# A convolution and squared-ReLU kernel: the tokens' scales as one row on every partition, applied ahead of the turning

## The chip, the cores and the metric

The kernel runs on one core of a Trainium2 chip. The metric is the device time of one execution in microseconds (us), here the median of three runs. A core has five engines with queues of their own that work side by side: TensorE (PE, matrix products; its weight loads are shown apart as PEld), VectorE (DVE), ScalarE (ACT), GpSimd (POOL) and SyncE (SP), which in this kernel issues every DMA. The transfers themselves run on 16 DMA engines.

## The reference

Eight sequences of 4096 tokens with 192 channels go through a convolution whose seven weights are made per token and head by a softmax, and then through a two-layer network with a squared ReLU between the layers:

```python
w = exp(weight_gen - max(weight_gen, -1)); w = w / (sum(w, -1) + 1e-9)   # [B, S, 8, 7]
x_unf = windows of 7 tokens ending at s, zeros ahead of token 0           # [B, S, 7, 8, 24]
out = einsum('bshk,bskhg->bshg', w, x_unf).reshape(B * S, 192)
h = out @ w_in                    # [32768, 192] @ [192, 2048]
r = maximum(h, 0.0)
result = ((r * r) @ w_out)        # [32768, 2048] @ [2048, 192], float32
```

Inputs and output are 32-bit floats (the network's two weight matrices arrive in 64 bits).

## The kernel before

**Tiling.** Partition p holds 256 consecutive tokens. A chunk `c` is four tokens of every partition (512 tokens); there are 64 chunks, and two chunks make a group `gi`, whose inputs one `load_group` brings in. Each matrix product is done with 16-bit operands: a number is split into a high and a low part (`xh`, `xl`; `gh`, `gl`; W and V hold split weights), and three products of parts are summed in PSUM.

**A chunk's path.** DVE makes the softmax weights and the seven products and sums of the convolution (`conv_steps`, L316 and L322). From chunk 4 on DVE also turns the sums in 32x32 blocks (L404), they go to DRAM and back (`xd`, L410 and L415), and arrive as `xT` with channels on partitions. ACT and DVE split `xT` into `xh` and `xl` (L356, L362). `mm1` (L440) makes the hidden layer in PSUM, ACT does ReLU, square and the high part (L447, L451, L455), DVE the low part (L459), and `mm2_turned` (L485, L489) multiplies by V. `finish` takes the sums out of PSUM to the tile `s` (L531 on ACT, L532 on DVE); `store_turned` turns `s` into `o_sb` (L548), multiplies by the tokens' scales (L550), and issues 24 stores of 16 KB (L557), whose pieces are 32 floats, 128 bytes.

**Turned chunks.** For chunks 4 to 62 (`turned(c)`) the products come out with channels on partitions and tokens along the row, so `s` is [128, 768] with 128 tokens in each of six blocks. Chunks 0 to 3 and 63 have tokens on partitions and take the scale as one number per partition, `falls[gi]` (L543, L544).

**The scales.** Each group's inputs are scaled by a power of two per partition, `ups`, and the output is brought back by `f`, which `descale(gi)` makes from `downs` and the weights' scale `back` (L152): one number for each of the 128 partitions, that is for each token place of a turned chunk. For groups 2 to 31 (30 groups) `descale` writes the 128 numbers from 128 partitions to a DRAM row `fd` of 512 bytes (L156), and reads them back four times (L158), once for each block of 32 partitions, so that partition i of a block has the numbers i, 32+i, 64+i and 96+i: the tile `fs`, [128, 4], which after the turning is what each output number needs.

**Order.** It is written out by hand. The loop at the end of the kernel runs over chunks and eight steps `b` in each: two `mm1`, the late low parts, `finish` and `store_turned` of the chunk before (at `b == 1`), a piece of `mm2`, then ACT's steps, then what `todo` holds for that step. `descale(gi)` stands there some three chunks ahead of the first chunk of its group. All DMAs stand in SP's one queue in the order in which they are written, and an instruction of SP that waits holds those behind it.

Of the kernel before, what the change touches and what calls it, by code (L numbers as in the profile page):

```python
# [8 lines left out]
F32 = mybir.dt.float32  # L9
# [4 lines left out]
ALU = mybir.AluOpType  # L14
# [15 lines left out]
def kernel(  # L30
# [9 lines left out]
    nc = tc.nc  # L40
# [4 lines left out]
    P = 128  # L45
    Q = 32
# [6 lines left out]
    CPG = TG // TC  # L53
# [8 lines left out]
    N_PE = 4  # L62
# [4 lines left out]
    att = ctx.enter_context(tc.tile_pool(name="att", bufs=1))  # L67
    xtp = ctx.enter_context(tc.tile_pool(name="xtp", bufs=2))
    gp = ctx.enter_context(tc.tile_pool(name="gp", bufs=4))
    op = ctx.enter_context(tc.tile_pool(name="op", bufs=2))  # L70
    dram = ctx.enter_context(tc.tile_pool(name="dram", bufs=2, space=bass.MemoryType.DRAM))
# [15 lines left out]
    back = const.tile([P, 1], F32, name="back")  # L87
# [3 lines left out]
    act, ts, tt = nc.scalar.activation, nc.vector.tensor_scalar, nc.vector.tensor_tensor  # L91
    stt = nc.vector.scalar_tensor_tensor
# [33 lines left out]
    sums, ups, downs, falls = {}, {}, {}, {}  # L126
# [20 lines left out]
    spread_falls = {}  # L147

    def descale(gi):
        f = falls[gi] = att.tile([P, 1], F32, name="f", bufs=3)  # L150
        d = downs.pop(gi)
        stt(out=f, in0=d, scalar=back, in1=d, op0=ALU.mult, op1=ALU.mult)  # L152
        if gi * CPG >= N_PE:
            fd = dram.tile([P], F32, name="fd")
            fs = spread_falls[gi] = att.tile([P, 1, P // Q, 1], F32, name="fs", bufs=3)
            nc.sync.dma_start(out=fd.rearrange("(p a) -> p a", a=1), in_=f)  # L156
            for m in range(P // Q):
                nc.sync.dma_start(  # L158
                    out=fs[m * Q:(m + 1) * Q, 0, :, 0], in_=fd.rearrange("(q i) -> i q", i=Q)
                )  # L160

    raws = {}

# [259 lines left out]
    def turned(c):  # L423
        return N_PE <= c < NCH - 1
# [96 lines left out]
    outs, sums_t = {}, {}  # L521
# [23 lines left out]

    def store_turned(c):
        o = op.tile([P, TC * D], F32, name="o_sb")
        nc.vector.transpose(o, sums_t.pop(c))  # L548
        ob = o.rearrange("p (a q j) -> p a q j", q=P // Q, j=Q)
        tt(out=ob, in0=ob, in1=spread_falls[c // CPG].broadcast_to(ob.shape), op=ALU.mult)  # L550
        for col in range(0, D, Q):
            for t in range(TC):
                if col < P:
                    p0, n0 = col, t * P
                else:
                    p0, n0 = 2 * t // TC * D1 + col - P, N + t % 2 * P
                nc.sync.dma_start(  # L557
                    out=out_v[:, c * TC + t, col:col + Q].rearrange("(q i) j -> i q j", i=Q),
                    in_=o[p0:p0 + Q, n0:n0 + P].rearrange("i (q j) -> i q j", j=Q),
                )  # L560
# [122 lines left out]
    cvt[NU][1]()  # L683
    cvt[NU][2]()
    descale(0)
    descale(1)
    for f in conv2[3:6]:
        f()
# [37 lines left out]
    for c in range(1, NCH + 1):  # L726
        for b in range(NB if c < NCH else 2):
            js = (2 * b, 2 * b + 1)
            if c < NCH:
                if b == 0 and c % 2 and (c + 3) // 2 * CPG < NCH:  # L730
                    load_group((c + 3) // 2)
                if c % 2 and b == 2 and (c + 3) // 2 * CPG < NCH:
                    total, scales = size_steps((c + 3) // 2)
                    b1 = 4 if c == 1 else 2
                    at(c, b1, total)
                    at(c, b1 + 1, scales)
                    at(c, b1 + 1, lambda gi=(c + 3) // 2: descale(gi))
                if b == 0 and c + 2 < NCH and c + 2 > 2:
                    plan_conv(c + 2)
                for j in js:  # L740
                    mm1(c, j)
# [6 lines left out]
            if b == 1:  # L748
                for p in range(2):
                    finish(c - 1, p)  # L750
                    if c == NCH:
                        store(c - 1, p, p + 1)
                if turned(c - 1):
                    store_turned(c - 1)
                elif c < NCH:
                    store(c - 1)
# [55 lines left out]
```

## Time and profile before

| | |
|---|---|
| median of three runs (2076.53 to 2078.67) | 2078.55 us |
| the profiled execution's own time | 2084.55 us |
| its span, first to last instruction | 2082.8 us |
| mean granted TensorE clock | 0.995 |
| busy: PE, PEld | 98%, 84% of the span |
| busy: DVE, ACT, POOL | 90%, 84%, 0% of the span |
| DMA: mean rate, share of the 16 engines that the kernel's queue used | 77 GB/s, 30.2% |

A row of a group of instructions reads: line, engine, operation, output<-inputs, shapes, count, then busy time in us, mean ns of one, and the engine's idle time just before them with what ended it. "issue" as a releaser means that the engine waited for nothing that the profile shows. In a row of a table by stretches of time, each engine's busy us (and number of instructions) stand in order PE, PEld, DVE, ACT, POOL, then the granted clock as a share of full speed, the share of the DMA engines and GB/s. In the list of DMA queues, q1 is the kernel's own transfers and q8, called "instruction", the loading of the engines' instructions.

### The profile page before, as it was taken

The numbers are of one execution on the slowest core, as the hardware profiler recorded it, in microseconds if no ns is written. First come the engines' busy times: TensorE is split into PE (matmuls) and PEld (weight loads), VectorE is DVE, ScalarE is ACT, GpSimd is POOL, SyncE is SP. The second block draws the span as 40 slices with busy tenths as digits, with TensorE's granted clock in tenths as the row PEclk, the third lists the DMA queues.
The fourth block names the chain that finished last, engine by engine and source line by source line (L and its number), as shares of the span: only waits on it lengthen the run. The fifth ranks groups of instructions, "written<-read, shape, count | busy, mean of one in ns | idle before, by whom it ended". The sixth has DMA issues, their size and how long they took to land.

```text
span 2082.8 us, 92659 instructions
## 1 busy us (share of the span) xinstructions
PE 2047.9 (98%) x42310; PEld 1744.4 (84%) x42310; DVE 1864.4 (90%) x2428; ACT 1750.4 (84%) x2010; POOL 10.2 (0%) x14
## 2 busy tenths in 40 slices
PE   8999999999999999999999999999999999999999
PEld 6776666678988889998888999998999988889886
DVE  8998999989999998999898999998899999999983
ACT  6788888878888888888888888887888888888887
POOL 1000000000000000000000000000000000000000
PEclk9999999999999999999999999999999999999999
DMA  6122233332323322233323233323332232332221
GB/s 183 40 71 69 56 83 79 95 81 49 86 68 94 92 75 61 66 85 94 85 60 73 68 95 90 76 56 86 72 92 74 55 89 70 94 90 72 59 59 23
DMA packets 315162, 159.71 MB, mean 77 GB/s; under 512 B 232729, under 2 KB 285337, under 8 KB 310801
## 3 DMA queue, kind: packets, MB, share of 16 engines
q1 hardware_dynamic: 314768, 153.79, 30.2%
q8 instruction: 330, 5.41, 1.3%
q14 instruction: 64, 0.52, 0.1%
HBM read 104.88 MB, written 48.77 MB: 74 GB/s over the span
## 4 chain that ended last, share of the span: by engine, by line
PE 95%; DVE 3%; issue 1%; SPq 0%; DMA 0%; ACT 0%; POOL 0%; DVEq 0%; POOLq 0%
PE ph L440 48%; PE acc L485 34%; PE acc L489 9%; PE acc L513 3%; DVE pr L316 1%; DVE pr L322 0%; DVE du L208 0%; DVE du L209 0%; DVE du L207 0%; PE ph L385 0%; DVE W L272 0%; SPq L117 0%; DMA xt<-in_x_dram 0%; DVE gl L459 0%; DVE xl L362 0%
## 5 line engine op out<-in xcount | busy, mean ns | idle before, releaser
L440 PEld LDWEIGHTS <-W 64*64 64x64 f16 (+1 forms) x17568 | 762.5, 107 | 208.7 <-issue 4.5
L440 PE MATMUL ph<-xh,W 64*64 64x512 f16 (+1 forms) x11712 | 882.7, 377 | 0.8 <-DVE xl L362 0.5
L485 PE MATMUL acc<-gh,V 64*64 64x512 f16 x7552 | 805.6, 377 | 13.4 <-issue 13.4
L459 DVE SCALAR_TENSOR_TENSOR gl<-gh,g 128x1024 f16<-128x1024 f16 x504 | 611.6, 1223 | 142.9 <-ACT gh L455 133.1
L447 ACT ACTIVATE g<-ph 128x1024 f32<-128x1024 f32 x504 | 511.9, 1016 | 258.0 <-PE ph L440 257.9
L485 PEld LDWEIGHTS <-V 64*64 64x64 f16 x11328 | 645.9, 107 | 76.1 <-issue 17.7
L489 PE MATMUL acc<-gh,V 64*64 64x256 f16 x7552 | 696.7, 270 | 4.1 <-issue 4.0
L489 PEld LDWEIGHTS <-V 64*64 64x64 f16 x11328 | 645.2, 107 | 22.7 <-issue 10.2
L451 ACT ACTIVATE g<-g 128x1024 f32<-128x1024 f32 x512 | 539.3, 1053 | 8.0
L455 ACT ACTIVATE gh<-g 128x1024 f16<-128x1024 f32 x504 | 530.7, 1053 | 8.0
L485 PE MATMUL acc<-gl,V 64*64 64x512 f16 x3776 | 497.8, 378 | 2.5 <-issue 2.5
L440 PE MATMUL ph<-xl,W 64*64 64x512 f16 (+1 forms) x5856 | 477.7, 377 | 0.0
L316 DVE TENSOR_TENSOR pr<-xt,wt 128x768 f32<-128x768 f32 x449 | 422.1, 953 | 2.8 <-DMA xt<-in_x_dram 0.7
L489 PE MATMUL acc<-gl,V 64*64 64x256 f16 x3776 | 395.7, 270 | 1.3 <-issue 1.3
L322 DVE TENSOR_TENSOR pr<-pr 128x768 f32<-128x768 f32 x384 | 365.3, 951 | 2.3
L362 DVE TENSOR_TENSOR xl<-xT,xh 128x512 f16<-128x512 f32 x180 | 113.5, 686 | 21.6 <-ACT xh L356 20.3
L356 ACT CAST xh<-xT 128x512 f16<-128x512 f32 x180 | 98.7, 611 | 1.2 <-DMA xT<-xd 1.1
L531 ACT COPY tmp<-acc 128x512 f32<-128x512 f32 x118 | 50.0, 475 | 24.3 <-PE acc L485 23.2
L532 DVE TENSOR_TENSOR s<-acc,tmp 128x512 f32<-128x512 f32 x118 | 60.0, 551 | 10.4 <-ACT tmp L531 10.4
L513 PE MATMUL acc<-V,gl 64*128 64x192 f16 x512 | 63.5, 243 | 2.9 <-issue 2.6
L513 PE MATMUL acc<-V,gh 64*128 64x192 f16 x1024 | 65.3, 243 | 0.0
L404 DVE STREAM_TRANSPOSE xr<-pr 128x768 f32<-128x768 f32 x60 | 58.7, 978 | 2.1
(76 smaller groups left out, 646.5 us busy)
## 6 DMA issues: line engine op xcount, KB each, us to landing
xT<-xd SPq DMA_DIRECT2D x120, 384.0 KB, 5.3
xt<-in_x_dram SPq DMA_DIRECT2D x31, 1344.0 KB, 6.9
xd<-xr SPq DMA_DIRECT2D x240, 96.0 KB, 3.5
out_dram<-o_sb SPq DMA_DIRECT2D x1416, 16.0 KB, 2.5
wt<-in_weight_gen_dram SPq DMA_DIRECT2D x31, 224.0 KB, 2.7
raw<-in_moe_w_in_dram SPq DMA_DIRECT2D x8, 384.0 KB
raw<-in_moe_w_out_dram SPq DMA_DIRECT2D x4, 768.0 KB, 4.4
fs<-fd SPq DMA_DIRECT2D x120, 0.5 KB, 4.0
```

The costliest lines, as they stand in the source:

```text
L316: tt(out=dst, in0=src, in1=wk.broadcast_to([P, (t1 - t0) * H, G]), op=ALU.mult)
L322: tt(out=prs[k0][:, part], in0=prs[k0][:, part], in1=prs[k][:, part], op=ALU.add)
L356: nc.scalar.copy(xh, xs)
L362: tt(out=xl, in0=xs, in1=xh, op=ALU.subtract)
L440: nc.tensor.matmul(ph[col, i], w[rows, k, j % 2, col], xx[rows, k], **fl)
L447: act(r, phs.pop((c, j)), AF.Relu, scale=RHO * LIFT ** 0.5)
L451: act(r, r, AF.Square)
L455: act(gh, rgs[c, j], AF.Copy, scale=1.0 / LIFT)
L459: stt(out=gl, in0=ghs[c, j], scalar=-LIFT, in1=rgs.pop((c, j)), op0=ALU.mult, op1=ALU.add)
L485: nc.tensor.matmul(accs[c][0][col, r], V[rows, fb, d:d + D1], g[rows, i], **fl)
L489: nc.tensor.matmul(accs[c][1][col, r, 0:N // 2], V[rows, fb, d:d + D1], g[rows, i, m * N // 2:(m + 1) * N // 2], **fl,)
L513: nc.tensor.matmul(accs[c][t // 2][:, h, t % 2 * D:(t % 2 + 1) * D], g[rows, i, t * P:(t + 1) * P], V[rows, fb, n * D:(n + 1) * D], start= ...
```

## The change

`descale` makes the scales 32 times side by side ([128, 32] instead of [128, 1]) and, for groups 2 to 31, turns that tile in 32x32 blocks on DVE, after which partitions 0, 32, 64 and 96 each hold 32 of the scales as a row. Four stores of one such row (32 floats, 128 bytes) each fill `fd`; one load brings `fd` back as a whole row of 128 numbers to each of the 128 partitions. `store_turned` multiplies `s` by that row, in place, and turns afterwards.

```diff
     def descale(gi):
-        f = falls[gi] = att.tile([P, 1], F32, name="f", bufs=3)
+        row = att.tile([P, Q], F32, name="f", bufs=3)
+        f = falls[gi] = row[:, 0:1]
         d = downs.pop(gi)
-        stt(out=f, in0=d, scalar=back, in1=d, op0=ALU.mult, op1=ALU.mult)
-        if gi * CPG >= N_PE:
-            fd = dram.tile([P], F32, name="fd")
-            fs = spread_falls[gi] = att.tile([P, 1, P // Q, 1], F32, name="fs", bufs=3)
-            nc.sync.dma_start(out=fd.rearrange("(p a) -> p a", a=1), in_=f)
-            for m in range(P // Q):
-                nc.sync.dma_start(
-                    out=fs[m * Q:(m + 1) * Q, 0, :, 0], in_=fd.rearrange("(q i) -> i q", i=Q)
-                )
+        dq = d.broadcast_to([P, Q])
+        stt(out=row, in0=dq, scalar=back, in1=dq, op0=ALU.mult, op1=ALU.mult)
+        if turned(gi * CPG):
+            turned_row = att.tile([P, Q], F32, name="ft", bufs=2)
+            nc.vector.transpose(turned_row, row)
+            fd = dram.tile([P // Q, Q], F32, name="fd")
+            for q in range(P // Q):
+                nc.sync.dma_start(out=fd[q:q + 1], in_=turned_row[q * Q:q * Q + 1, :])
+            fs = spread_falls[gi] = att.tile([P, 1, P], F32, name="fs", bufs=3)
+            nc.sync.dma_start(
+                out=fs[:, 0], in_=fd.rearrange("(a q) i -> a (q i)", a=1).broadcast_to([P, P])
+            )
...
     def store_turned(c):
         o = op.tile([P, TC * D], F32, name="o_sb")
-        nc.vector.transpose(o, sums_t.pop(c))
-        ob = o.rearrange("p (a q j) -> p a q j", q=P // Q, j=Q)
-        tt(out=ob, in0=ob, in1=spread_falls[c // CPG].broadcast_to(ob.shape), op=ALU.mult)
+        sm = sums_t.pop(c)
+        sb = sm.rearrange("p (t n) -> p t n", n=P)
+        tt(out=sb, in0=sb, in1=spread_falls[c // CPG].broadcast_to(sb.shape), op=ALU.mult)
+        nc.vector.transpose(o, sm)
```

The order of PE's and ACT's instructions is as before. On SP, at one group's `descale` (the rows stand between the output stores of one chunk and the DRAM trip of a later one), before:

```order
L557 DMA out_dram<-o_sb 32x4x32 x24
L156 DMA fd<-f 128x1
L158 DMA fs<-fd 32x4x1 x4
L410 DMA xd<-xr 32x6x128 x4
L415 DMA xT<-xd 64x3x512 x2
```

and now:

```order
L562 DMA out_dram<-o_sb 32x4x32 x24
L160 DMA fd<-ft 1x32 x4
L162 DMA fs<-fd 128x128
L414 DMA xd<-xr 32x6x128 x4
L419 DMA xT<-xd 64x3x512 x2
```

One store and four loads have become four stores and one load, at the same place of the queue. On DVE, at the same `descale` (`down` and `up` are the group's powers of two, `gl` the low part of the hidden layer, `pr` the convolution's products), before:

```order
L142 TENSOR_SCALAR down<-down 128x1
L96 TENSOR_SCALAR up<-down 128x1
L97 TENSOR_SCALAR down<-down 128x1
L152 SCALAR_TENSOR_TENSOR f<-down,back 128x1
L459 SCALAR_TENSOR_TENSOR gl<-gh,g 128x1024 x2
```

and now:

```order
L142 TENSOR_SCALAR down<-down 128x1
L96 TENSOR_SCALAR up<-down 128x1
L97 TENSOR_SCALAR down<-down 128x1
L154 SCALAR_TENSOR_TENSOR f<-down,back 128x32
L157 STREAM_TRANSPOSE ft<-f 128x32
L463 SCALAR_TENSOR_TENSOR gl<-gh,g 128x1024 x2
```

The first is wider, and a transpose of [128, 32] has come in behind it. In `store_turned` the two DVE instructions of 128x768 have changed places, the multiplication (L554, formerly L550) now ahead of the transpose (L555, formerly L548).

## The prediction

> **What bounds the kernel now.** I read the page's first part, then the table of waits, then the stretches of time around one group's `descale`, and last the DMA list. The busy times and PE's waits:
>
> ```profile
> PE 2047.9 (98%) x42310; PEld 1744.4 (84%) x42310; DVE 1864.4 (90%) x2428; ACT 1750.4 (84%) x2010; POOL 10.2 (0%) x14
> PE acc L485 <- issue: 15.8, 11, 2.6
> PE acc L489 <- issue: 5.3, 5, 1.9
> PE acc L513 <- issue: 2.6, 1, 2.6
> core 0: 2082.8 us, clock 0.995
> ```
>
> PE is the bound. Behind the start it waits for no other engine to speak of: what it loses is "issue", 15.8 + 5.3 + 2.6 = 23.7 us in 17 gaps of up to 2.6 us, and the clock, which was granted at 0.995 in the mean, 0.005 x 2082.8 = 10.4 us. So the question is where these gaps stand. I cut the time into 30 stretches from 5.5 to 9.5 us behind each issue of the store `fd<-f`, and the 29 stretches between them. Three of the short ones, their sum, the sum of the long ones, and the stretch behind the gap at 424:
>
> ```profile
> 361.10:365.10 4.00, 4.00 (x100) 2.47 (x92) 3.93 (x6) 3.72 (x6) 0.00 (x0) 1.00 0.05 4
> 423.40:427.40 4.00, 2.09 (x41) 1.12 (x33) 3.93 (x6) 2.94 (x4) 0.00 (x0) 0.96 0.00 0
> 805.60:809.60 4.00, 1.37 (x33) 1.08 (x28) 3.93 (x6) 2.93 (x4) 0.00 (x0) 0.97 0.01 4
> sum 120.00, PE 95.82 PEld 77.66 DVE 117.86 ACT 102.02 POOL 0.00; mean PE 3.19 PEld 2.59 DVE 3.93 ACT 3.40 POOL 0.00
> sum 1719.10, PE 1719.10 PEld 1485.60 DVE 1555.19 ACT 1462.48 POOL 0.00; mean PE 59.28 PEld 51.23 DVE 53.63 ACT 50.43 POOL 0.00
> 427.05:430.46 3.41, 3.41 (x44) 2.90 (x48) 1.41 (x3) 0.85 (x2) 0.00 (x0) 0.50 0.04 0
> ```
>
> In the 120 us just ahead of the landing of `fd`, PE is idle for 24.2; in the other 1719.1 us it is never idle. After a gap the clock may stand at half for 3.41 us (last row). Every gap of the steady state thus belongs to the store of the scales. How it does so is seen at 417.90 (SP's and PE's timeline) and in the DMA list of 418.0 to 426.7, followed by the list's rows for the whole run:
>
> ```profile
> 417.90 0.34 SPq L156 DMA_DIRECT2D fd<-f  x1
> 424.34 0.38 PE L485 MATMUL acc<-gl,V 64*64 64x512 f16 x1
> 426.34 0.37 PE L485 MATMUL acc<-gl,V 64*64 64x512 f16 x1 [1.63 <-issue]
> 427.01 1.74 SPq L158 DMA_DIRECT2D fs<-fd  x4
> ...
> DMA packets 145, 0.02 MB, mean 2 GB/s; under 512 B 144, under 2 KB 144, under 8 KB 144
> q8 instruction: 1, 0.02, 2.4%
> q1 hardware_dynamic: 144, 0.00, 0.9%
> ...
> q8 instruction: 330, 5.41, 1.3%
> out_dram<-o_sb SPq DMA_DIRECT2D x1416, 16.0 KB, 2.5
> fs<-fd SPq DMA_DIRECT2D x120, 0.5 KB, 4.0
> fd<-f SPq DMA_DIRECT2D x30, 0.5 KB, 8.7
> ```
>
> The store of 512 bytes takes 8.7 us to land, longer than any other transfer of its size or of 32 times its size: `o_sb` stores 16 KB in pieces of 128 bytes in 2.5 us. Its pieces are 4 bytes (144 packets: 128 and some 16 for the end). Meanwhile the DMA engines move nothing but one packet of instructions, which needs 2.4% of 16 engines over 8.7 us, 3.3 us; over the run 1.3% x 16 x 2082.8 / 330 makes 1.3 us a packet. The 330 packets carry the program's 92,659 instructions, about 280 each; PE executes 48 per us (x100 and x92 in the 4.00 us from 361.10), so a packet is some 6 us of its work. So while the small writes are outstanding instructions are held up, and PE runs dry. The earliest it did:
>
> ```profile
> 800.08 0.34 SPq L156 DMA_DIRECT2D fd<-f  x1
> 808.72 0.42 PE L485 MATMUL acc<-gh,V 64*64 64x512 f16 x2 [2.63 <-issue]
> ```
>
> 808.72 - 2.63 - 800.08 = 6.0 us behind the issue: a hold-up that ends before 6.0 us should cost PE nothing, and one of 8.7 us at most 2.7, as the longest gaps show.
>
> **What the hold-up costs in all.** Rather than add gaps, clock and restarts, I take the distance between issues of `fd`, one group of PE work:
>
> ```profile
> 164.56 0.34 SPq L156 DMA_DIRECT2D fd<-f  x1
> 231.06 0.34 SPq L156 DMA_DIRECT2D fd<-f  x1
> 293.34 0.34 SPq L156 DMA_DIRECT2D fd<-f  x1
> 484.52 0.34 SPq L156 DMA_DIRECT2D fd<-f  x1
> 1948.94 0.34 SPq L156 DMA_DIRECT2D fd<-f  x1
> ```
>
> A group without a gap takes 293.34 - 231.06 = 62.28 us (so do 10 more of the 28); the one from 417.90 to 484.52, with 1.9 us of gaps, takes 66.62. From the first to the last are 28 groups, 1784.38 us; at 62.28 each they would take 1743.84. The loss is 40.5 us: 24.2 idle, about 10 of clock, and some 6 of slow restart around the gaps.
>
> By the Trainium skill (TensorE: Matmul & The Clock Gate, Part 1) the clock falls after an idle window of about 3.4 us; by that rule no gap here would lower it and the loss would be the 30 us of idling and restart, an estimate of 2048.5. The trace differs: the clock was at 0.50 behind a gap of 1.63 us, so the rows decide.
>
> **The change, part by part.** *The stores.* Gone are the 128 pieces of 4 bytes; four stores of one 128-byte piece come instead. The trace has no store from a single partition. The nearest row is `o_sb`, pieces of the same 128 bytes, 2.5 us to landing, though there are 128 of them. At 0.34 us an issue the fourth starts 1.0 us behind the first and lands at about 3.5. From above: if a store to `fd` lands in 8.7 us whatever its pieces, the last lands at about 1.0 + 8.7 = 9.7. I take 3.5, since the piece is the same as `o_sb`'s and during 24 of those stores in a row PE never idles. That is under 6.0, and the stores cost PE nothing.
>
> *The load.* One broadcast of 512 bytes to 128 partitions instead of four gathers that land in 4.0 us at the median. It moves 64 KB in 512-byte pieces; `o_sb`'s quarter of that lands in 2.5. I take 4; it is issued when the stores have landed, so it is done about 8 us behind the first issue. Gathers of the same row run without a gap in the 29 long stretches, which hold them all, so I count no hold-up from reading. `fs` is used some three chunks (over 90 us) later and is not waited for.
>
> *SP's queue* holds what stands behind the load: the next chunk's `xd` and `xT`, and later the output stores. They now wait for the landing of four stores (about 3.5 us) instead of one. How long SP waited before, with the rows for DVE's part:
>
> ```profile
> SPq L158 <- DMA fd<-f: 231.6, 29, 8.7
> ACT xh L356 <- DMA xT<-xd: 1.1, 1, 1.1
> L303 DVE TENSOR_SCALAR sm<-sm 128x32 f32<-128x32 f32 x64 | 11.6, 181 | 2.2
> L152 DVE SCALAR_TENSOR_TENSOR f<-down,back 128x1 f32<-128x1 f32 x32 | 6.9, 220 | 1.1
> L142 DVE TENSOR_SCALAR down<-down 128x1 f32<-128x1 f32 x31 | 4.8, 154 | 1.1
> L548 DVE STREAM_TRANSPOSE o_sb<-s 128x768 f32<-128x768 f32 x59 | 57.7, 978 | 2.0
> L550 DVE TENSOR_TENSOR o_sb<-o_sb,fs 128x768 f32<-128x768 f32 x59 | 56.5, 958 | 2.0
> L316 DVE TENSOR_TENSOR pr<-xt,wt 128x768 f32<-128x768 f32 x447 | 421.1, 955 | 2.8 <-DMA xt<-in_x_dram 0.7
> ```
>
> 231.6 us of SP's waiting shrink by some 4 to 5 us per group. Nobody gains: `xT` was waited for once, 1.1 us. Nor is anything behind it made later.
>
> *DVE.* The scales' instruction grows from 128x1 to 128x32: between L142 (154 ns) and L303 (181) lie the same 31 elements, so 220 becomes about 247. The new transpose of 128x32 costs between 154 ns and the 978 of 128x768; near the small end, 0.2 us. Together 0.23 us in 62.28, 30 x 0.23 = 7 us in all, on an engine that is idle 120 - 117.9 + 1719.1 - 1555.2 = 166 us of these stretches; PE, busy without a break in the long stretches beside it, does not wait for DVE. Were that cover gone, the price would be those 7 us. In `store_turned` a multiplication (958) and a transpose (978) change places; the second operand now repeats in the middle dimension, and L316's (955) repeats inside, so the rate does not depend on that. Zero.
>
> **The sum.** 2084.55 - 40.5 = 2044.0 for the profiled execution. It stands 6.0 us over the median of the runs. If those 6 us are a fixed cost of being profiled, the runs come to 2038; if they are hold-ups that the runs have less of, 2044. Between them 2041; I add 2 for groups in which the stores and the load together still starve PE: **2043 us**.
>
> **The rivals.** *A part remains.* If the load holds instructions up as the store did, the hold-up ends at 8 us instead of 8.7: gaps of at most 2.0 instead of 2.7, and since both their number and their length shrink, about (2.0/2.7) squared = 0.55 of the loss stays, 22 us: 2078.55 - 18.5 = 2060. Against it: the gathers, which hold none up.
>
> *Nothing happens.* The gaps stand where `descale` stands, but something else of that moment could starve PE, the DVE or ACT work around it for one. Then 2078.55. The Trainium skill (Runtime: NRT & Kernel Launch, Instruction fetch mechanics) calls the crossing into the next block of instructions mostly hidden, which speaks for this rival. Against it: a packet of instructions at 3.3 us instead of 1.3, and a gap in the middle of four like products whose operands are there.
>
> *Slower.* The 8.7 us belong to the target, a row of 512 bytes that all pieces share, not to the 4-byte piece; then four stores, issued over 1.0 us, land at 9.7, and later still if they queue up at the row. A hold-up to 9.7 makes gaps up to 3.7, a loss of 40.5 x (3.7/2.7) squared = 76 us, so 2078.55 + 35.5 = 2114. The point from which it decides is 8.7 us from the first issue to the last landing. For it: `fd` has no other kind of write in this trace. Against it: stores of 128-byte pieces elsewhere at 2.5 us.
>
> **How the numbers follow.** 0.68 for the loss gone (2036 to 2050), 0.15 for a part remaining (2050 to 2070), 0.10 for nothing, 0.07 for slower. A measurement of this kernel tells about 0.2%, 4 us, from no change. Faster than 2074.4: 0.68 + 0.15 + 0.02 of the third case = 0.85; same 0.08; slower 0.07. The range reaches from 2036 (all of it, and a little more) to 2066, into the case of a part remaining.
>
> **What would show it.** Right: the landing of the new stores at 2 to 3 us each; the 4 us stretches behind them with PE at 4.00; PE's "issue" waits near zero behind the start; a mean clock of 0.999 or 1.000; groups 62.28 us apart throughout; instruction packets near their 1.3 us at `descale`. Wrong: stores at 8 us, gaps still ending 8 to 9 us behind the first issue, or DVE appearing among what PE waits for. The number would be wrong with all steps right if the unprofiled runs lose less, or more, to the hold-up than this profile does.

## The result, and the profile after

The changed kernel takes 2043.58 us (median of four runs, 2043.23 to 2043.75); the kernel before, run beside it, 2078.61. The ratio is 0.9834, with a 95% interval of 0.9817 to 0.9851: 1.7% faster, 35 us.

The page of the changed kernel, PE's table of waits in full, and the rows of its stretches. These are cut as before: 30 stretches from 5.5 to 9.5 us behind the first store of each group (two of them and their sum) and the 29 between them (their sum):

```profile
PE 2030.9 (99%) x42310; PEld 1281.5 (63%) x42310; DVE 1865.1 (91%) x2458; ACT 1748.2 (86%) x2010; POOL 10.8 (1%) x14
core 0: 2041.7 us, clock 1.000
PE ph L580 <- POOL ident masks.py:199: 2.4, 1, 2.4
PE acc L389 <- DVE pr L326: 1.8, 2, 1.4
PE ph L444 <- ACT xT L354: 1.2, 1, 1.2
PE ph L389 <- DVE pr L326: 0.7, 1, 0.7
PE ph L444 <- DVE xl L366: 0.5, 1, 0.5
PE acc L517 <- DVE gl L463: 0.3, 1, 0.3
...
232.70:236.70 4.00, 4.00 (x96) 2.52 (x92) 3.93 (x6) 3.41 (x6) 0.00 (x0) 1.00 0.23 52
1914.20:1918.20 4.00, 4.00 (x96) 2.52 (x92) 3.93 (x6) 3.47 (x6) 0.00 (x0) 1.00 0.30 72
sum 120.00, PE 120.00 PEld 76.22 DVE 117.81 ACT 101.51 POOL 0.00; mean PE 4.00 PEld 2.54 DVE 3.93 ACT 3.38 POOL 0.00
sum 1678.20, PE 1678.20 PEld 1043.59 DVE 1556.24 ACT 1460.43 POOL 0.00; mean PE 57.87 PEld 35.99 DVE 53.66 ACT 50.36 POOL 0.00
```

No wait on "issue" is left, and what PE still waits for lies in the start of the program. The 4 us stretches in which it idled 24.2 us before are full, and the clock is at 1.000. SP's timeline around some of the groups, its wait for the stores, the DMA list, and DVE's new rows:

```profile
165.21 1.11 SPq L160 DMA_DIRECT2D fd<-ft  x4
167.22 0.34 SPq L162 DMA_DIRECT2D fs<-fd  x1
227.19 1.12 SPq L160 DMA_DIRECT2D fd<-ft  x4
229.34 0.35 SPq L162 DMA_DIRECT2D fs<-fd  x1
289.47 1.12 SPq L160 DMA_DIRECT2D fd<-ft  x4
1908.75 1.12 SPq L160 DMA_DIRECT2D fd<-ft  x4
...
SPq L162 <- DMA fd<-ft: 23.6, 40, 0.9
...
q8 instruction: 330, 5.41, 1.2%
L154 DVE SCALAR_TENSOR_TENSOR f<-down,back 128x32 f32<-128x32 f32 x32 | 8.0, 251 | 1.1
L157 DVE STREAM_TRANSPOSE ft<-f 128x32 f32<-128x32 f32 x30 | 6.4, 212 | 1.0
L554 DVE TENSOR_TENSOR s<-s,fs 128x768 f32<-128x768 f32 x59 | 56.5, 958 | 2.0
L555 DVE STREAM_TRANSPOSE o_sb<-s 128x768 f32<-128x768 f32 x59 | 57.7, 978 | 2.0
```

The load, which waits for the four stores, is issued 2.0 to 2.2 us behind the first of them in these groups, so they have landed by then. From 165.21 to 1908.75 are 28 groups, 1743.54 us, 62.27 each in the mean: every group now takes what only the undisturbed ones took before (the first of them 61.98, the others 62.27 to 62.29). The 28 groups took 1784.38 us; the 40.8 us between the two are the whole difference of the spans, 2082.8 - 2041.7 = 41.1.

### The profile page after: what moved, and what is told of

Read it like the earlier page. It is cut to its first block, busy times and chain, and to the rows that moved or that the text cites. A ratio compares the mean times of both kernels' runs of the same rounds, so it can differ in the third digit from the quotient of the medians.

```text
span 2041.7 us, 92661 instructions
## 1 busy us (share of the span) xinstructions
PE 2030.9 (99%) x42310; PEld 1281.5 (63%) x42310; DVE 1865.1 (91%) x2458; ACT 1748.2 (86%) x2010; POOL 10.8 (1%) x14
## 4 chain that ended last, share of the span: by engine, by line
PE 98%; DVE 1%; DMA 0%; SPq 0%; issue 0%; ACT 0%; POOL 0%; ACTq 0%; POOLq 0%
PE ph L444 49%; PE acc L489 30%; PE acc L493 15%; PE acc L517 3%; PE acc L476 1%; DMA raw<-in_moe_w_in_dram 0%; PE ph L389 0%; DVE W L276 0%; DVE pr L320 0%; SPq L180 0%; SPq L117 0%; DVE pr L326 0%; DVE gl L463 0%; DVE xl L366 0%; ACT xh L360 0%
## 5 line engine op out<-in xcount | busy, mean ns | idle before, releaser
L444 PEld LDWEIGHTS <-W 64*64 64x64 f16 (+1 forms) x17568 | 522.5, 107 | 428.6 <-issue 1.2
L444 PE MATMUL ph<-xh,W 64*64 64x512 f16 (+1 forms) x11712 | 781.1, 376 | 0.5 <-DVE xl L366 0.5
L489 PE MATMUL acc<-gh,V 64*64 64x512 f16 x7552 | 671.2, 376 | 0.0
L493 PE MATMUL acc<-gh,V 64*64 64x256 f16 x7552 | 526.8, 269 | 0.0
L489 PEld LDWEIGHTS <-V 64*64 64x64 f16 x11328 | 331.3, 107 | 280.2 <-issue 0.4
L444 PE MATMUL ph<-xl,W 64*64 64x512 f16 (+1 forms) x5856 | 411.9, 376 | 0.0
L489 PE MATMUL acc<-gl,V 64*64 64x512 f16 x3776 | 364.4, 376 | 0.0
L493 PEld LDWEIGHTS <-V 64*64 64x64 f16 x11328 | 331.3, 107 | 23.2
L493 PE MATMUL acc<-gl,V 64*64 64x256 f16 x3776 | 263.4, 269 | 0.0
L555 DVE STREAM_TRANSPOSE o_sb<-s 128x768 f32<-128x768 f32 x59 | 57.7, 978 | 2.0
```

Of the source, the lines that this page charges most:

```text
L444: nc.tensor.matmul(ph[col, i], w[rows, k, j % 2, col], xx[rows, k], **fl)
L489: nc.tensor.matmul(accs[c][0][col, r], V[rows, fb, d:d + D1], g[rows, i], **fl)
L493: nc.tensor.matmul(accs[c][1][col, r, 0:N // 2], V[rows, fb, d:d + D1], g[rows, i, m * N // 2:(m + 1) * N // 2], **fl,)
```

## The experiments

The kernel before ran again beside each set of experiments. There, on three chips, it took 2062 to 2063 us rather than 2079; the gain to be explained is 20 us in them. All comparisons below are with the runs of the same set.

**The old store in the changed kernel.**

```diff
-            turned_row = att.tile([P, Q], F32, name="ft", bufs=2)
-            nc.vector.transpose(turned_row, row)
             fd = dram.tile([P // Q, Q], F32, name="fd")
-            for q in range(P // Q):
-                nc.sync.dma_start(out=fd[q:q + 1], in_=turned_row[q * Q:q * Q + 1, :])
+            nc.sync.dma_start(out=fd.rearrange("q (i a) -> (q i) a", a=1), in_=f)
```

> The changed kernel with the old store alone: 128 pieces of 4 bytes from 128 partitions into the 512-byte row; the broadcast load, and the multiplication ahead of the turning, stay as changed. Theory S (the store of 4-byte pieces holds the instruction packets up, and nothing else in the change matters): about 2078 us, gaps of PE 6 to 9 us behind the store. Rival L (the four gathers of 4 bytes, gone here too, are part of the hold-up): between 2044 and 2070, with fewer gaps. Rival M (the order of multiplication and turning gave the gain): 2044.

2060.35 us against 2063.14, ratio 0.998 (0.9969 to 0.9991). **The new stores in the kernel before:**

```diff
+            turned_row = att.tile([P, Q], F32, name="ft", bufs=2)
+            nc.vector.transpose(turned_row, row)
-            nc.sync.dma_start(out=fd.rearrange("(p a) -> p a", a=1), in_=f)
+            for q in range(P // Q):
+                nc.sync.dma_start(out=fd[q:q + 1], in_=turned_row[q * Q:q * Q + 1, :])
```

(with `row` made 32 wide as in the change; the gathers and `store_turned` are those of before.)

> The kernel before with the new stores alone: the scales made 32 wide and turned, four stores of 128 bytes; the four gathers of 4-byte pieces and the order in store_turned as before. Theory S: 2044 us, PE's issue waits zero in the steady state, groups 62.28 us apart. Rival L: 2050 to 2075, with gaps behind the gathers. Rival M: 2078.

2043.03 us, ratio 0.9898 (0.9869 to 0.9926), no "issue" wait of PE. The two runs mirror each other: with the old store the rest of the change gains 2.8 of 20 us, with the new stores all 20 us are there without the rest. Theory S holds for the change as it is. The 2.8 us are clear of noise, since their interval ends at 0.9991, and they stay unexplained: the gathers, which are gone here, may own them while the old store stands, but beside the new stores they cost nothing. PE's waits with the old store in the changed kernel, and its row of the DMA list:

```profile
PE acc L486 <- issue: 6.9, 7, 2.2
PE acc L490 <- issue: 2.9, 4, 1.2
PE acc L514 <- issue: 1.8, 1, 1.8
fd<-f SPq DMA_DIRECT2D x30, 0.5 KB, 7.3
```

The 7.3 us rest on one of the 30 stores, the only one for which the list has a landing. The load, which waits for the store, is issued 7.2 to 9.4 us behind it, 7.8 in the mean.

**Pieces of 128 bytes from 128 partitions**, without turning:

```diff
-            fd = dram.tile([P], F32, name="fd")
-            nc.sync.dma_start(out=fd.rearrange("(p a) -> p a", a=1), in_=f)
+            fd = dram.tile([P, Q], F32, name="fd")
+            nc.sync.dma_start(out=fd, in_=row)
```

> The kernel before with the scales made 32 wide and stored without turning: 128 pieces of 128 bytes from 128 partitions, to 16 KB of DRAM, of which the gathers read the first number of each. Theory P (it is the size of the piece: 4 bytes are slow, 128 are not) and theory T (it is the shared row of 512 bytes, which takes one small write after another): both a store that lands in 2 to 3 us and 2044 us. Rival N (128 pieces from 128 partitions are slow whatever their size): 8 us to landing and 2078 us.

2043.27 us, ratio 0.9899 (0.987 to 0.9928). **Pieces of 4 bytes, 512 bytes apart:**

```diff
-            fd = dram.tile([P], F32, name="fd")
-            nc.sync.dma_start(out=fd.rearrange("(p a) -> p a", a=1), in_=f)
+            fd = dram.tile([P, P], F32, name="fd")
+            nc.sync.dma_start(out=fd[:, 0:1], in_=f)
```

(the gathers read `fd[:, 0:1]`.)

> The kernel before with its 128 pieces of 4 bytes written 512 bytes apart (64 KB of DRAM instead of one row of 512 bytes); the gathers read them there. Theory P (the size of the piece): landing at about 8.7 us, 2078 us. Theory T (the shared row): landing at 2 to 4 us, 2044 us. In the trace of before the last eight of the store's engines finish between 4.4 and 9.1 us behind the issue, one after the other, about 0.7 us apart, which speaks a little for T.

2042.99 us, ratio 0.9897 (0.9869 to 0.9926). The DMA list's rows for `fd` of the two, wide pieces first:

```profile
fd<-f SPq DMA_DIRECT2D x30, 16.0 KB, 1.9
```

```profile
fd<-f SPq DMA_DIRECT2D x30, 0.5 KB, 2.3
```

Theory P falls. Pieces of 4 bytes are as quick as pieces of 128 when they are apart, and neither the number of pieces nor of partitions makes them slow. What was slow is many small pieces close together.

**How near is one place?** The kernel before with its 4-byte pieces 64, 16 and 8 bytes apart, which is one number in the tile's shape (the store and the gathers are those of the pieces 512 bytes apart):

```diff
-            fd = dram.tile([P, P], F32, name="fd")
+            fd = dram.tile([P, 16], F32, name="fd")    # 64 bytes apart
+            fd = dram.tile([P, 4], F32, name="fd")     # 16 bytes apart
+            fd = dram.tile([P, 2], F32, name="fd")     # 8 bytes apart
```

and 8-byte pieces that touch, from a scale made two wide:

```diff
+        row = att.tile([P, 2], F32, name="f", bufs=3)
...
+            fd = dram.tile([P, 2], F32, name="fd")
+            nc.sync.dma_start(out=fd, in_=row)
```

With them the kernel before again, for its profile.

> The kernel before, unchanged, for its profile beside the next three: in the runs of the first experiments it took 2063 us instead of 2079. If the loss is the hold-up by the store, the landing of fd and the number of gaps are smaller wherever the time is, and the distances between groups without a gap stay 62.28 us.

> The kernel before with its 128 pieces of 4 bytes written 64 bytes apart, 8 KB in all, eight pieces in each 512 bytes; the gathers read them there. If pieces hinder each other within 512 bytes or a wider row: landing well over e4's 2.3 us, towards before's. If only within 64 bytes or less: 2.3 us and 2043.5 us.

> The kernel before with its 128 pieces of 4 bytes written 16 bytes apart, 2 KB, four pieces in each 64 bytes. One piece in 64 bytes landed in 1.4 us, sixteen in about 8: theory T64 gives (8 - 1.4)/15 = 0.44 us for each further piece, 2.7 us here; no gaps, since that is under 6.0 us: 2043 us. Rival (only pieces that touch each other are slow): 1.4 us.

> The kernel before with its 128 pieces of 4 bytes written 8 bytes apart, 1 KB, eight pieces in each 64 bytes. Theory T64: 1.4 + 7 x 0.44 = 4.5 us to landing, still under 6.0 us, no gaps: 2043 us. If hold-ups cost in proportion (rival R of the half store) about 40% of the loss of before, 2051. Rival (only pieces that touch each other are slow): 1.4 us, 2043.

> The kernel before with two equal scales side by side on each partition, stored as 128 pieces of 8 bytes that touch each other, 1 KB, eight pieces in each 64 bytes; the gathers read the first of each two. Four bytes 8 bytes apart, also eight in 64 bytes, landed in 3.0 us at the median. Theory C (what counts is how many pieces fall into the same 64 bytes, or 32): about 3 us, no gaps, 2043 us. Theory A (pieces that touch each other are slow, since the 4-byte pieces of before are the only ones so far that touch within 64 bytes): 6 to 9 us, gaps, 2050 to 2063.

| `fd` written as | pieces in 64 bytes | landing, us | time, us | ratio to before (95%) |
|---|---|---|---|---|
| 4 bytes, 64 apart | 1 | 1.4 | 2042.95 | 0.9903 (0.9875 to 0.9932) |
| 4 bytes, 16 apart | 4 | 2.4 | 2043.06 | 0.9913 (0.989 to 0.9935) |
| 4 bytes, 8 apart | 8 | 3.0 | 2043.27 | 0.9911 (0.9888 to 0.9933) |
| 8 bytes, touching | 8 | 3.1 | 2043.01 | 0.9905 (0.9882 to 0.9927) |
| 4 bytes, touching (before) | 16 | 8 (see below) | 2063.27 | 1.0002 (0.9991 to 1.0013) |

The DMA list's rows behind the landings, in the table's order:

```profile
fd<-f SPq DMA_DIRECT2D x30, 0.5 KB, 1.4
```

```profile
fd<-f SPq DMA_DIRECT2D x30, 0.5 KB, 2.4
```

```profile
fd<-f SPq DMA_DIRECT2D x30, 0.5 KB, 3.0
```

```profile
fd<-f SPq DMA_DIRECT2D x30, 1.0 KB, 3.1
```

Touching as such does not matter (theory C, not A); sixteen pieces in 64 bytes do. Nor do they hinder each other by a fixed time each: one to four pieces lie between 1.4 and 2.4 us in no clear order (512 bytes apart took 2.3), eight take 3.0, sixteen about 8. The 0.44 us a piece of theory T64 gave 4.5 for eight, so that theory is wrong in its law. (Single landings of the pieces 16, 64 and 512 bytes apart scatter from 1.4 to 3.7 us in all three runs, so the order of their medians says little.) Whether the place is 64 or 32 bytes wide, and why the last step is so much larger than the one before, stays open. So does whether the number of pieces counts or the number of DMA engines that write them: the semaphore that tells of the landing of one such store rises sixteen times in the trace, as many times as there are DMA engines. If each rise is one engine's share, an engine has eight pieces, and eight in 64 bytes may come from one engine, sixteen from two. The repeated profile of before (PE's waits; the waits of SP; SP's and PE's timeline at its first group with a gap):

```profile
PE acc L485 <- issue: 9.9, 10, 1.9
PE acc L489 <- issue: 2.7, 5, 1.0
PE acc L513 <- issue: 2.0, 1, 2.0
SPq L158 <- DMA fd<-f: 197.4, 27, 7.9
164.37 0.34 SPq L156 DMA_DIRECT2D fd<-f  x1
172.38 1.74 SPq L158 DMA_DIRECT2D fs<-fd  x4
172.36 0.24 PE L513 MATMUL acc<-V,gl 64*128 64x192 f16 x1 [1.97 <-issue]
core 0: 2061.3 us, clock 1.000
```

The load, which waits for the store, is issued 8.0 us behind it (172.38 - 164.37), where the first profile had 8.2 at the same group and 9.1 at 417.90. Over the 30 stores it is 7.7 us in the mean (7.0 to 8.3) against 8.4 (7.7 to 9.1) in the first profile. The gaps are shorter, 14.6 us in all, and no half clock follows them. PE again runs dry 172.36 - 1.97 - 164.37 = 6.0 us behind the store. So a landing shorter by 0.7 us went with half the loss. The gaps stand at the same places of the program: 13 of the 14 stores with a gap behind them had one in the first profile as well.

**Half and double the pieces, in a store that nobody reads**, added to the changed kernel behind its four stores:

```diff
+            fx = dram.tile([64, 1], F32, name="fx")
+            nc.sync.dma_start(out=fx, in_=row[0:64, 0:1])
```

```diff
+            fx = dram.tile([2, P], F32, name="fx")
+            nc.sync.dma_start(
+                out=fx.rearrange("n p -> p n"),
+                in_=row[:, 0:4].rearrange("p (n two) -> p n two", two=2)[:, :, 0],
+            )
```

> The changed kernel with an extra store behind the four: 64 numbers of 4 bytes from 64 partitions into one row of 256 bytes that nobody reads. By the last run 4-byte pieces are slow only when they share a row; between e4's 2.3 us to landing and the 8.7 of before lie 128 pieces at 50 ns, so 64 pieces land at about 5.5 us. Theory H (a hold-up costs nothing until PE's store of instructions is used up, 6.0 us): 2044 us, at most a gap or two. Rival R (the loss goes in proportion to the time of the hold-up): half of what before loses beside 2043.5, some 10 to 17 us.

> The changed kernel with an extra store of 256 numbers of 4 bytes into 1 KB that nobody reads: two rows of 512 bytes, each of 128 pieces. If the rows are served one after the other: landing at 2.3 + 256 x 50 ns = 15 us, and by theory H each of the 30 groups has a gap of between 3 and 9 us, mean 6, and the half clock behind it (1.7): some 30 x 8 = 240 us, about 2280. If the rows are served side by side: landing as before, the loss of before, 2060 to 2080. If the extra store is harmless since nobody waits for it (rival W: SP's waiting for fd is what hurts): 2044.

2057.26 us (ratio to the kernel before 0.9976, 0.9962 to 0.9989) and 2087.66 us (1.012, 1.0091 to 1.0149), where the changed kernel would take some 2043.5. PE's waits, half and double:

```profile
PE ph L446 <- issue: 3.6, 5, 1.5
PE acc L491 <- issue: 3.5, 3, 1.4
PE acc L495 <- issue: 2.2, 2, 1.5
SPq L164 <- DMA fd<-ft: 6.9, 29, 0.3
```

```profile
PE ph L449 <- issue: 16.5, 13, 3.6
PE acc L498 <- issue: 8.6, 4, 2.3
PE acc L494 <- issue: 3.6, 2, 2.1
SPq L167 <- DMA fd<-ft: 10.1, 30, 0.4
```

SP waits for nothing of this store, and the loss is there: rival W falls, it is the writing and not SP's waiting. The sizes I expected were wrong on both sides. Half the pieces cost 14 us, not nothing, and double the pieces 44, not 240. Both keep 16 pieces in every 64 bytes. The extra store's semaphore shows when it landed, although nothing waits for it: 7.2 us behind the issue in the mean with 64 pieces (the 13 stores of which the trace has all sixteen rises) and 8.3 with 256 (5 stores, 7.7 to 9.6), where the 128 pieces of before took 7.6 on the same chip (13 stores). So the landing grows far more slowly than the number of pieces while sixteen of them share 64 bytes: places side by side are mostly served together, and the 50 ns a piece of the expectations are refuted. Theory H is not refuted by the 14 us, since the store with half the pieces lands beyond 6.0 us and not at 5.5, but this run does not test it. The runs that do are the two with eight pieces in 64 bytes: 3 us of hold-up, no gap, where rival R has 2051.

**One DMA engine.** The kernel before, its store cut into 127 partitions and one:

```diff
-            nc.sync.dma_start(out=fd.rearrange("(p a) -> p a", a=1), in_=f)
+            fp = fd.rearrange("(p a) -> p a", a=1)
+            for lo, hi in ((0, P - 1), (P - 1, P)):
+                nc.sync.dma_start(out=fp[lo:hi], in_=f[lo:hi])
```

> The kernel before with its store cut in two, 127 partitions and 1, into the same 512 bytes. By the Trainium skill (DMA: Bandwidth & Descriptors, Why a DMA increments its semaphore by 16 and not by 1) a copy of 127 rows runs on one DMA engine, not on 16; the time will tell. Theory T64 (small writes into the same 64 bytes are done one after the other, wherever they come from): landing at 8 us or later, as before. If the memory itself keeps the instruction packets waiting, gaps and the loss of before, about 2060; if it is the queue of the engine that writes, gaps only for packets on that engine, 2044 to 2055. Rival E (several engines writing into the same 64 bytes hinder each other): one engine alone lands in 2 to 4 us, 2043.5.

2083.61 us, ratio 1.0101 (1.0071 to 1.013). SP's timeline and PE's waits:

```profile
226.28 1.00 SPq L158 DMA_DIRECT2D fd<-f  x2
235.38 3.42 SPq L160 DMA_DIRECT2D fs<-fd  x4
...
PE acc L487 <- issue: 12.9, 7, 2.4
PE acc L491 <- issue: 9.8, 6, 2.3
PE ph L442 <- issue: 4.7, 5, 1.8
```

The loads follow 9.1 us behind the first store here, 9.3 in the mean of the 30 groups (7.7 in the repeated profile of before, which is from another chip), and the loss is 40 us where the kernel before, on this chip, loses 20. Rival E, with its 2 to 4 us, is not borne out, if 127 partitions do run on one engine; the profile does not name engines, so that rests on the Trainium skill (DMA: Bandwidth & Descriptors, Why a DMA increments its semaphore by 16 and not by 1). The trace agrees: the semaphore of this store rises 0.4 us behind the issue and then once more, at 8.5 to 9.5 us (19 stores whose landing the trace holds), where that of the store from 128 partitions rises up to sixteen times between 2.1 and 9.1 us. The records of the DMA packets have all the pieces taken up within 1.6 us of the issue, so the time is not spent in taking them from the queue, which speaks for the memory's side. But no run has one engine write 127 pieces that lie apart, so one engine's writing may be slow by itself, and rival E is not excluded. And a queue that the instructions share with that one engine would hold them up as the memory would. Both are left open.

**Is it the loading of instructions?** That the crowded store makes the gaps is shown: its spacing alone removes them. That it does so through the loading of instructions is argued. In the first profile of before 26 of the 330 packets of instructions take more than 2 us, up to 4.1, and each of them starts within 10 us behind a store `fd<-f`; all others take 1.8 or less, as do all 330 in the changed kernel. PE's gaps end between 1.1 us before and 0.5 us behind the issue of the load, that is about when the store has landed. But the trace does not tell whose instructions a packet carries, and the slow packets do not tell where a gap will be: 13 of the 14 stores without a gap have one behind them as well, and 6 of the 16 with a gap have none that starts before the gap ends. So a cause that goes with the store and that the profile does not show is not excluded.

## Why the prediction was right

*The time*: 2043 us forecast, 2043.58 measured, in a range of 2036 to 2066.

*What bounds the kernel* was read rightly: all gaps of PE belonged to the store of the scales, and with it the "issue" waits, the half clock and the slow restarts went together. The term of the sum, 40.5 us for 28 groups, measured 40.8 (the first of them takes 61.98 us undisturbed, not 62.28); the profiled execution was forecast at 2044.0 and took 2043.75.

*The 6 us* between the profiled execution of before and its runs: of the two readings the second held. The changed kernel's profiled execution lies 0.2 us from its median, so profiling has no fixed cost here, and the runs of before lost less to the hold-up than the profiled execution did. The 2 us added for groups that would still starve were not needed. That 2043 came so near is luck in part: the middle of the two readings was too low by about what the addition was too high.

*The stores*: the 8.7 us to the landing of the old store stand on three of the 30 stores, the only ones for which the list has a landing; the load that waits for it is issued after 7.7 to 9.1 us, 8.4 in the mean, which changes nothing in the sum. For the new stores 3.5 us was taken to the last landing; all four have landed by the issue of the load, at 2.0 to 2.2 us. The reason given was wrong in part. I set the piece of 128 bytes against the piece of 4, and the runs show 4 bytes just as quick when they are apart. The slower rival named the better cause, a target that all pieces share, but drew from it that four stores would be slow as well. What counts, in the runs above, is how many pieces fall into the same 64 bytes (or how many engines write there), and four whole 128-byte pieces share none. The kernel before with 4-byte pieces 8 bytes apart is as fast as the change.

*6.0 us* as the time from the store to PE's earliest idling came back in the second profile of before, and fits the runs with 3 us of hold-up. The square of what exceeds it, which priced two rivals, gives (2.0/2.7) squared = 0.55 for the gaps of up to 1.97 us in that profile. Between the spans the loss is 2061.3 - 2041.7 = 19.6 there against 41.1, or 0.48, between the runs 20 against 35, or 0.57.

*The load, SP, DVE*: the broadcast holds nothing up; instruction packets take 1.2% x 16 x 2041.7 / 330 = 1.2 us. The wide instruction costs 251 ns (247 forecast), the small transpose 212 (200), and multiplication and transpose 958 and 978 in either order. By the run with only the stores changed, all else in the change is worth nothing that can be measured beside the new stores (beside the old one it was worth 2.8 us).

*Nothing happens* was wrong: the gaps went with the store. The Trainium skill's "mostly hidden" (Runtime: NRT & Kernel Launch, Instruction fetch mechanics) does not hold for this kernel while such a store is under way, if the loading of instructions is what PE waits for: in the run with the extra store of 256 numbers, which no instruction waits for, PE's gaps that end on "issue" came to over 28 us.

## What to carry to other kernels

When a saturated engine shows gaps whose releaser is "issue", look at what stands at a fixed distance ahead of them; here one DMA of 512 bytes, which no engine waited for, cost up to 2%, most likely by holding up the loading of instructions. Small numbers from many partitions should not be written next to each other in DRAM: padding behind each (64 bytes apart in one run; here 8 bytes apart was already enough) does as much as turning them into long pieces first, and costs no instruction. The distance between repeats of the same instruction in undisturbed and disturbed groups gave the loss better than adding up gaps, clock and restarts.

## What the runs showed of the hardware that was not expected

- 128 writes of 4 bytes to DRAM land in 1.4 to 2.4 us at the median when at most four share 64 bytes, in 3.0 when eight do, and in about 8 when sixteen do. With sixteen the landing depends little on how many there are in all: 64 took 7.2 us, 256 took 8.3.
- While such writes are outstanding, packets of instructions can take 2 to 4 us instead of 0.9 to 1.8, though the engines move almost nothing else.
- The same kernel lost 35 us in one set of runs and about 20 in four others, with landings that differ by 0.7 us between the two profiles. By the mean time to the landing, or to the load that waits for it, there is no loss at 3 us, 14 us at 7.2, 17 to 20 at 7.7 to 7.8, 41 to 44 at 8.3 to 8.4, and no more than 40 where the load came at 9.3.
- PE's weight loads were busy for 1744.4 us before and 1281.5 after, the same 42310 of them. The groups without a gap take 62.28 us in both, so it costs nothing there; why it is so was not tried.
